# A three-stage transformer kernel: transfers of the expert arms issued by GpSimd, late conversions moved into the last arm, transposes ahead of the second unit

## The chip, the cores and the metric

One Trainium2 chip, one of its cores. The metric is the device time of one execution in microseconds (us). Five engines run their own instruction streams and meet at semaphores: TensorE (PE, with its weight loads PEld), VectorE (DVE), ScalarE (ACT), GpSimd (POOL) and SyncE (SP). SP computes nothing here: it issues transfers. A transfer issued by SP goes to queue q1 (hardware), one issued by POOL to queue q0 (software).

## The reference, cut to what matters

```python
attn_out = softmax(causal(q @ k.T / sqrt(64))) @ v        # B 4, H 12, S 448, D 64
x = attn_out -> rows (1792, 768)

def _moe_ref(x, w_gate, w_output_gate, w1, w2):           # 8 experts, 768 -> 1024 -> 768
    e_idx = np.argmax(x @ w_gate, axis=1)                 # one expert for each row
    for e in range(E):
        h = np.maximum(x[mask] @ w1[e], 0.0)
        out[mask] = gate_w * eom * (h @ w2[e])

def _moe2_ref(x, w_in, w_out):                            # 768 -> 2048 -> 768, weights float64
    h = x @ w_in
    g = h - np.tanh(h)
    return g @ w_out
```

How many rows an expert gets is known only on the chip, so the number of row blocks of each expert is a register value and the extra blocks are conditional. The weights of the second network come as float64 and must be turned into two float16 planes (a high and a low one).

## The kernel before

**Three stages.** Attention runs to about 240 us. The experts follow, one after the other, to about 539 us. Then the second network runs to the end, first as the hidden tiles `fh` (L1358) of row group 0, which DVE and ACT pace, then as `fo` (L1409) and `fh` together, which keep PE full.

**An expert** `e` has one block of 128 rows that is always computed, the main slot `slot(e, FB[e], ...)`, and then nested conditional arms, `extra(e, i)`: each is a `tc.If(cntr > i)` with one more slot in it. A slot is a first product (`ph`, L164), a relu that splits it in a high and a low half (`hh` on ACT L171, `hl` on DVE L172), a second product (`py`, L176) and the result `yo` (ACT L893), which is stored to `ys_d` (L921). All engines branch at an arm (L934). With this input the following arms are taken (the stores of `ys_d` in the trace show it): none for experts 0, 3 and 5, one for experts 1, 4 and 7, two for expert 2, four for expert 6.

**What the main slots carry besides.** While expert `e` is computed, the weights of the next one come in: SP issues 14 loads `raw<-w` (L107) in the order in which they are used, ACT makes the high plane `w` (L115), DVE the low one (L123). SP runs ahead of PE by the three staging buffers `raw`.

**What the arms carry besides.** Each arm converts "units" of the float64 weights: a load `cu<-wf` of 1 MB (`conv_load`, L971), three DVE steps that build a float32 (`to_f32`, L961, L964, L967), the high planes on ACT (L115), the low planes on DVE (L123) or on POOL (`rest_of` with "p": L117 and L131), and a store `wb_d<-co` of 512 KB (`conv_store`, L988). Arms of experts 1 to 5 have two units, those of expert 6 three. There are two load buffers `cu`, so a unit's load is issued when the float32 step of the unit that had the buffer before is done. The third unit of expert 6's arms takes the low planes on POOL. `conv_fill(e, i)` calls these steps at the points `z` = 0 to 4 of the slot. The row numbers of loads and stores come from a table through a register (`unit_of`, L999), read on SP.

**An arm that is not taken.** The program was scheduled as if the arm ran, so each engine that skips it still has to bring the semaphores up to the counts that the transfers in it would have left. In the trace these are the rows of L934: the branch itself, `EVENT_SEMAPHORE` on SP and `INC_SWDGE_SEM` on POOL.

**Expert 7** has no next expert. Its main slot has a `fill` of its own: the last units of the arms, `prep_max` (row maxima, L1064), `first_planes`, `first_hi` and `first_rest`, which prepare row group 0 of the second network (scales, high planes, low planes `prep_lo`, L1092). After its arm comes the **junction** to the second network: the transposes of group 0 (`prep2`: PE L151, copies L153 and L155), the row scales (`prep3`: `rsp`, L1134 and L1135), the two last units (loads into `stg[0]` and `stg[1]`, converted in place), and the scales of group 1 (`prep1`, `prep_sc`, L1072 to L1110, and `prep_hi`, ACT L1084). In the loop behind it, step `a_mm(n)` makes `fh` and `act_a(n)` takes it from PSUM to `cc` (DVE L1366), then ACT L1367 to L1374, POOL L1368 and L1371 and DVE L1378 work on it.

The order of an engine's instructions is the order in which the code is written; nothing reorders them later.

## Time and profile before

| | |
|---|---|
| median of 3 runs | 1016.27 us (1013.7 to 1017.19) |
| profiled execution | 1012.6 us, span 1010.9 us |
| mean granted TensorE clock | 0.989 |
| PE busy | 961.9 us, 95% |
| DVE, ACT, POOL busy | 791.5, 614.3, 480.9 us |

The span is the part of the execution that the trace covers; 1.7 us lie around it. In the trace's lists a row gives its start, its time, the engine, the line, what is written and read, and in brackets how long the engine had been idle before it and what released it. "SPq" or "ACTq" is the engine's own sequencer, that is a branch, a register read or a semaphore step. The granted clock 1.00 is the upper of TensorE's two levels (2.4 GHz), 0.50 the lower (1.2 GHz).

### The profile page before, as it was taken

The numbers are of one execution on the slowest core, as the hardware profiler recorded it, in microseconds if no ns is written. First come the engines' busy times: TensorE is split into PE (matmuls) and PEld (weight loads), VectorE is DVE, ScalarE is ACT, GpSimd is POOL, SyncE is SP. The second block draws the span as 40 slices with busy tenths as digits, with TensorE's granted clock in tenths as the row PEclk, the third lists the DMA queues.
The fourth block names the chain that finished last, engine by engine and source line by source line (L and its number), as shares of the span: only waits on it lengthen the run. The fifth ranks groups of instructions, "written<-read, shape, count | busy, mean of one in ns | idle before, by whom it ended". The sixth has DMA issues, their size and how long they took to land. (4 is left out here: it accounts for less than half of the span.)

```text
span 1010.9 us, 24113 instructions
## 1 busy us (share of the span) xinstructions
PE 961.9 (95%) x9177; PEld 715.8 (71%) x9177; DVE 791.5 (78%) x1740; ACT 614.3 (61%) x1174; POOL 480.9 (48%) x544
## 2 busy tenths in 40 slices
PE   4999999998999999989998899999999999999996
PEld 3998989986878787768684555666666666667764
DVE  7888888977978686876886999886988788686640
ACT  5898988764654556643354897665665665565530
POOL 8668887863211111302255797554534544343321
PEclk9999999999999999989998999999999999999998
DMA  9777787577799989879875340010001000000000
GB/s 243 219 230 215 217 225 191 178 244 252 276 388 347 308 330 352 314 244 344 309 269 226 125 194 17 32 32 10 29 27 33 17 24 8 17 17 16 17 24 24
DMA packets 59831, 166.36 MB, mean 165 GB/s; under 512 B 7920, under 2 KB 21872, under 8 KB 56608
## 3 DMA queue, kind: packets, MB, share of 16 engines
q1 hardware_dynamic: 55120, 144.68, 43.0%
q0 software_dynamic: 4560, 19.80, 5.5%
q8 instruction: 80, 1.31, 0.5%
q14 instruction: 71, 0.58, 0.2%
HBM read 122.21 MB, written 29.62 MB: 150 GB/s over the span
## 5 line engine op out<-in xcount | busy, mean ns | idle before, releaser
L1409 PE MATMUL fo<-wo,g 128*128 128x384 f16 x1344 | 228.2, 326 | 0.0
L1358 PEld LDWEIGHTS <-raw 128*128 128x128 f16 x1440 | 142.2, 99 | 86.9 <-issue 10.3
L1409 PEld LDWEIGHTS <-g 128*128 128x128 f16 x1344 | 131.2, 98 | 83.8
L1368 POOL TENSOR_TENSOR V<-cu,cc 128x384 f32<-128x384 f32 (+1 forms) x80 | 78.5, 982 | 190.7 <-ACT cu L1367 189.7
L164 PEld LDWEIGHTS <-w 128*128 128x128 f16 x2592 | 145.9, 98 | 8.5 <-issue 7.4
L1358 PE MATMUL fh<-cu,raw 128*128 128x384 f16 (+1 forms) x864 | 135.6, 314 | 3.5 <-DVE cc L1366 2.6
L123 DVE SCALAR_TENSOR_TENSOR w<-raw,w 128x768 f16<-128x768 f32 (+1 forms) x99 | 100.2, 1073 | 8.0 <-ACT w L115 8.0
L371 ACT ACTIVATE P<-s,nb 112x112 f32<-112x112 f32 (+1 forms) x192 | 91.5, 510 | 22.2 <-DVE nb L363 20.1
L858 POOL DMA_INDIRECT xg<-xs_d,idx x22 | 32.8, 1490 | 148.5 <-PEq L934 28.6
L115 ACT ACTIVATE w<-raw 128x768 f16<-128x768 f32 (+2 forms) x106 | 90.0, 908 | 12.2 <-DMA raw<-w 10.7
L1367 ACT ACTIVATE cu<-cc 128x384 f32<-128x384 f32 (+1 forms) x80 | 40.1, 501 | 94.1 <-DVE cc L1366 94.1
L363 DVE CUSTOM_DVE_ANT_0 s<-s,maskw 112x112 f32<-112x112 f32 (+1 forms) x192 | 86.2, 455 | 9.6 <-PE s L357 5.5
L1371 POOL TENSOR_TENSOR X<-cc,X 128x384 f32<-128x384 f32 (+1 forms) x80 | 91.2, 1140 | 4.2 <-ACT X L1370 0.5
L1366 DVE TENSOR_TENSOR cc<-fh,co 128x384 f32<-128x384 f32 (+1 forms) x80 | 42.0, 525 | 64.7 <-PE fh L1358 51.9
L1378 DVE SCALAR_TENSOR_TENSOR V<-cu,V 128x384 f32<-128x384 f32 (+1 forms) x80 | 85.1, 1063 | 0.1
L420 PE MATMUL o<-v,PT 112*112 112x65 f32 x576 | 83.9, 269 | 0.0
L1386 DVE TENSOR_TENSOR V<-V,co 128x384 f32<-128x384 f32 (+1 forms) x64 | 78.4, 1224 | 0.0
L1387 ACT ACTIVATE g<-V 128x384 f16<-128x384 f32 (+1 forms) x80 | 40.1, 502 | 47.1 <-DVE V L1386 47.0
L1358 PE MATMUL fh<-yh,raw 128*128 128x384 f16 x384 | 67.6, 326 | 0.7 <-DVE cc L1366 0.7
L420 PEld LDWEIGHTS o<-v,PT 112*112 112x112 f32 x576 | 67.8, 177 | 0.0
L390 PE MATMUL t<-ident,P 112*112 112x112 f32 x480 | 67.0, 262 | 0.0
L356 PE MATMUL s<-kh,qa 128*112 128x112 f16 (+1 forms) x192 | 53.2, 298 | 13.1 <-POOL qa L293 7.1
(678 smaller groups left out, 2096.8 us busy)
## 6 DMA issues: line engine op xcount, KB each, us to landing
raw<-w SPq DMA_DIRECT2D x48, 512.0 KB
raw<-w SPq DMA_DIRECT2D x64, 384.0 KB
cu<-wf SPq DMA_DIRECT2D x22, 1024.0 KB
wb_d<-co SPq DMA_DIRECT2D x22, 512.0 KB
raw<-kq SPq DMA_DIRECT2D x11, 896.0 KB
raw<-wb_d SPq DMA_DIRECT2D x8, 768.0 KB
xs_d<-xq SPq DMA_DIRECT2D x24, 224.0 KB
raw<-v SPq DMA_DIRECT2D x11, 448.0 KB
```

Source lines behind the costliest of these rows:

```text
L115: nc.scalar.activation(out=out, in_=in_, func=AF.Copy, scale=WS)
L123: nc.vector.scalar_tensor_tensor(out=out, in0=in_, scalar=WS, in1=hi, op0=ALU.mult, op1=ALU.subtract)
L164: nc.tensor.matmul(out=ph[:, (f % 4) * 128 : (f % 4 + 1) * 128], lhsT=w[0][:, ww, k, f * 128 : (f + 1) * 128], rhs=xTs[tag][:, xx, k, :], ...
L363: nc.vector.tensor_tensor_reduce(out=d["s", m][:, z, :], in0=d["s", m][:, z, :], in1=maskw[:, S - n : S], scale=-0.125, scalar=3.0e38, op0 ...
L371: nc.scalar.activation(out=d["P"][:, j, OFF[i] : OFF[i] + n], in_=d["s", m][:, z, :], func=AF.Exp, bias=d["nb"][:, 2 * i + j : 2 * i + j + ...
L420: nc.tensor.matmul(out=po[:, i, :], lhsT=d["PT"][:, PT_AT[g], o : o + CP], rhs=d["t"][3][:, hl, j, :], start=(j == 0), stop=(j == i))
L1358: nc.tensor.matmul(out=ph[:, 0:nt], lhsT=wi[ww][:, f // 4, k, f % 4 * 128 : (f % 4 + 1) * 128], rhs=yy[:, k, 0:nt], start=(q == 0), stop=( ...
L1368: nc.gpsimd.tensor_tensor(out=d["V"], in0=d["U"], in1=d["h"], op=ALU.mult)
L1371: nc.gpsimd.tensor_tensor(out=d["X"], in0=d["h"], in1=d["X"], op=ALU.subtract)
L1378: nc.vector.scalar_tensor_tensor(out=d["V"], in0=d[f"S{z}"], scalar=QD[z - 1], in1=d["V"], op0=ALU.add, op1=ALU.mult)
L1386: nc.vector.tensor_tensor(out=d["V"], in0=d["V"], in1=rs_y(g, nt), op=ALU.mult)
L1409: nc.tensor.matmul(out=po[:, 0:384], lhsT=t[:, x, k, i * 128 : (i + 1) * 128], rhs=wo_[ww][:, k, z * 384 : (z + 1) * 384], start=(k == 0 a ...
```

## The change

Three things are edited. In the arms, the loads and stores of the units and the store of the slot's result are issued by POOL and no longer by SP, and the registers for them are read on POOL; a main slot's own store stays on SP. In expert 7, `prep_max(0)` moves from before the first product to point 1 of the main slot, `first_rest` makes all three low planes on DVE (two were on POOL) and moves with the conversion of the first of the two last units into the arm, or into an `Else` branch if the arm isn't taken. At the junction, the transposes of group 0 stand first, then the second of the last units, and the scales of group 1 move behind `act_a(0)` of the loop.

```diff
--- before.py
+++ after.py
@@ -20,6 +20,7 @@
 AX = mybir.AxisListType
 PSUM = bass.MemoryType.PSUM
 SP = mybir.EngineType.SP
+POOL = mybir.EngineType.Pool
 
 B, H, S, D = 4, 12, 448, 64
 CP, NCH = 112, 4
@@ -914,11 +915,12 @@
         out_z(1, py)
         j = i - FB[e]
         if isinstance(j, int) and j == 0:
-            cstr[0] = nc.values_load(cst0[0:1, e : e + 1], engines=(SP,), min_val=0, max_val=NT)
-            r0 = cstr[0]
+            r0 = nc.values_load(cst0[0:1, e : e + 1], engines=(SP,), min_val=0, max_val=NT)
+            nc.sync.dma_start(out=ys_d[ds(r0, 128)], in_=yo)
+            cstr[0] = nc.values_load(cst0[0:1, e : e + 1], engines=(POOL,), min_val=0, max_val=NT)
         else:
-            r0 = nc.snap(cstr[0] + j * 128, engines=(SP,), min_val=0, max_val=NT)
-        nc.sync.dma_start(out=ys_d[ds(r0, 128)], in_=yo)
+            r0 = nc.snap(cstr[0] + j * 128, engines=(POOL,), min_val=0, max_val=NT)
+            nc.gpsimd.dma_start(out=ys_d[ds(r0, 128)], in_=yo)
         fill(4)
 
     cstr = [None]
@@ -931,16 +933,20 @@
     def extra(e, i, w):
         last = FB[e] + LV
         nxt = (i + 1) % 2
-        with tc.If(cntr > i, label=f"more_{e}_{i}"):
+        with tc.If(cntr > i, label=f"more_{e}_{i}") as more:
             hint(e, i + 1)
             if i > last:
                 beyond(e, i, w)
                 return
             if e == E - 1 and 1 < i < last:
                 slot_rows(e, i + 1, 0)
-            slot(e, i, w, i % 2, conv_fill(e, i), trans=((0, nxt),) if i < last else (),
+            slot(e, i, w, i % 2, last_fill if e == E - 1 and i == 1 else conv_fill(e, i), trans=((0, nxt),) if i < last else (),
                  then=(lambda: slot_rows(e, i + 2, 0),) if i + 1 < last and e + 1 < E else (), late=True)
             extra(e, i + 1, w)
+        if e == E - 1 and i == 1:
+            with more.Else():
+                for z in range(5):
+                    last_fill(z)
 
     def beyond(e, i0, w):
         icol = mt.tile([128, 1], U32, name=f"icol_{e}", tag="icol", bufs=1)
@@ -984,8 +990,8 @@
 
     stores = []
 
-    def conv_store(b, r):
-        st = nc.sync.dma_start(out=wb_d[:, :, ds(r, 1), :].rearrange("p a o n -> p a (o n)"), in_=co[b]).ins
+    def conv_store(b, r, eng=nc.sync):
+        st = eng.dma_start(out=wb_d[:, :, ds(r, 1), :].rearrange("p a o n -> p a (o n)"), in_=co[b]).ins
         tc.declare_no_dep(st, group="units", reason="each unit has a place of its own in wb_d")
         tc.add_to_no_dep_group("units", st)
         stores.append(st.name)
@@ -995,8 +1001,8 @@
             tc.add_manual_dep(ins, n, mybir.DependencyInfo(mybir.DependencyClass.Sync, mybir.DependencyReason.DATA),
                               reason="reads what the stores of the units wrote")
 
-    def unit_of(e, n):
-        return nc.values_load(xtab[0:1, UOFF[e] + n : UOFF[e] + n + 1], engines=(SP,), min_val=0, max_val=NDY - 1)
+    def unit_of(e, n, eng=SP):
+        return nc.values_load(xtab[0:1, UOFF[e] + n : UOFF[e] + n + 1], engines=(eng,), min_val=0, max_val=NDY - 1)
 
     def conv_fill(e, i):
         c = CPE[e] if e + 1 < E else 0
@@ -1010,8 +1016,8 @@
                 if z == at:
                     conv(cu[b], co[b][:, 0], co[b][:, 1], "p" if j == 2 else "v")
                 if z == (4 if at == 3 else at):
-                    conv_load(cu[b], unit_of(e, n0 + j + min(c, 2)))
-                    conv_store(b, unit_of(e, n0 + j))
+                    conv_load(cu[b], unit_of(e, n0 + j + min(c, 2), POOL), nc.gpsimd)
+                    conv_store(b, unit_of(e, n0 + j, POOL), nc.gpsimd)
 
         return fill
 
@@ -1156,8 +1162,8 @@
         prep_dg(0, 0, GB[0])
 
     def first_rest():
-        for j in range(GB[0] - 1):
-            prep_lo(0, 0, GB[0], j, "p")
+        for j in range(GB[0]):
+            prep_lo(0, 0, GB[0], j)
 
     def rows_again(step):
         for g in range(2):
@@ -1253,11 +1259,8 @@
             second = nc.values_load(flg[0:1, 0:1], engines=(SP,), min_val=0, max_val=128)
             remaining()
             qc = (cc, wof[0][:, 8192:10240].bitcast(U32))
-            prep_max(0, 0, GB[0], (0, 1))
 
             def fill(z):
-                if z == 0:
-                    prep_max(0, 0, GB[0], (2,))
                 if z == 2:
                     first_hi()
                 if z in (1, 2):
@@ -1267,10 +1270,28 @@
                 if z == 1:
                     for q in range(2):
                         conv_load(stg[q], NDY + q, nc.gpsimd)
+                    prep_max(0, 0, GB[0])
                     first_planes()
                 if z == 3:
+                    prep_max(1, 0, GB[1])
+
+            qhl = [[y[:, (10 + q) * 1024 : (11 + q) * 1024] for y in wof] for q in range(2)]
+
+            def last_f32(q):
+                to_f32([(qc[q][:, h], stg[q][:, h, :]) for h in HS])
+
+            def last_planes(q):
+                for z in range(2):
+                    for h in HS:
+                        c = qc[q][:, h].bitcast(F32)
+                        scaled("a", qhl[q][0][:, h], c) if z == 0 else rest_of("p", qhl[q][1][:, h], c, qhl[q][0][:, h])
+
+            def last_fill(z):
+                if z == 1:
+                    last_f32(0)
                     first_rest()
-                    prep_max(1, 0, GB[1])
+                if z == 2:
+                    last_planes(0)
 
         slot(e, FB[e], wts[e], f"n{e % 2}", fill,
              ((1, (FB[e] + 1) % 2),) + ((("n", f"n{(e + 1) % 2}"),) if e + 1 < E else ()),
@@ -1306,23 +1327,12 @@
         extra(e, 1 + FB[e], wts[e])
         if e == 0:
             conv_load(cu[1], unit_of(1, 1))
-    qhl = [[y[:, (10 + q) * 1024 : (11 + q) * 1024] for y in wof] for q in range(2)]
-    prep_lo(0, 0, GB[0], GB[0] - 1)
-    for q in range(2):
-        to_f32([(qc[q][:, h], stg[q][:, h, :]) for h in HS])
-        for z in range(2):
-            for h in HS:
-                c = qc[q][:, h].bitcast(F32)
-                scaled("a", qhl[q][0][:, h], c) if z == 0 else rest_of("p", qhl[q][1][:, h], c, qhl[q][0][:, h])
-        if q == 0:
-            for prep in (prep2, prep3):
-                for i in range(GB[0]):
-                    tpool[0] = (mp_t, mp_y, mp_h)[i]
-                    prep(0, i, "tys"[i])
-    prep1(1, 0, GB[1], False, False)
-    prep_sc(1, 0, GB[1])
-    for j in (2, 0, 1):
-        prep_hi(1, 0, GB[1], j)
+    for prep in (prep2, prep3):
+        for i in range(GB[0]):
+            tpool[0] = (mp_t, mp_y, mp_h)[i]
+            prep(0, i, "tys"[i])
+    last_f32(1)
+    last_planes(1)
 
     mctx.close()
     gt = [w16s[1][z].tile([128, 2, KF2, 384], F16, tag=tg, name=f"g_{z}") for z, tg in enumerate(("w1", "w2"))]
@@ -1443,6 +1453,11 @@
             act_c(n - 2, 1)
         if okf(n - 3):
             act_d(n - 3)
+        if n == 0:
+            prep1(1, 0, GB[1], False, False)
+            prep_sc(1, 0, GB[1])
+            for j in (2, 0, 1):
+                prep_hi(1, 0, GB[1], j)
         if n in (1, 2, 3):
             prep_lo(1, 0, GB[1], (2, 0, 1)[n - 1])
         if n == 4:
```

The first rows are SP's, at the end of expert 5's main slot and at its first arm; `cst_82` is the register of the main slot's store, `xtab` the table of unit numbers. Before:

```order
L107 DMA raw_90<-w 128x768 x8
L917 TENSOR_LOAD cst_82
L917 ISA x2
L921 ISA
L921 DMA ys_d<-yo_I-14134_14135 128x768
L934 COMPARE_AND_BRANCH
L929 REGISTER_ALU
L1511 BRANCH_PREFETCH_HINT
L999 TENSOR_LOAD xtab
L999 ISA x2
L971 ISA
L971 DMA cu_4988<-wf 128x2048
```

The same place in the changed kernel:

```order
L108 DMA raw_90<-w 128x768 x8
L918 TENSOR_LOAD cst_82
L918 ISA x2
L919 ISA
L919 DMA ys_d<-yo_I-14184_14185 128x768
L936 COMPARE_AND_BRANCH
L931 REGISTER_ALU
L1526 BRANCH_PREFETCH_HINT
```

SP's arms are empty now: behind these rows stand only the branches of the further arms, and then the loads for the next expert but one.

The second place is POOL's stream at the end of expert 6's first arm: the low planes of the third unit. Before:

```order
L858 DMA xg_4589<-xs_d,idx 128x1536
L117 TENSOR_SCALAR scm<-cc 128x512
L131 TENSOR_TENSOR co_4991<-scm,co_4991 128x512
L117 TENSOR_SCALAR scm<-cc 128x512
L131 TENSOR_TENSOR co_4991<-scm,co_4991 128x512
L934 COMPARE_AND_BRANCH
```

In the changed kernel:

```order
L994 DMA wb_d<-co_5002 256x1x1024
L118 TENSOR_SCALAR scm<-cc 128x512
L132 TENSOR_TENSOR co_5001<-scm,co_5001 128x512
L118 TENSOR_SCALAR scm<-cc 128x512
L132 TENSOR_TENSOR co_5001<-scm,co_5001 128x512
L922 ISA
L923 DMA ys_d<-yo_I-16475_16476 128x768
L1005 TENSOR_LOAD xtab
L1005 ISA x2
L977 ISA
L977 DMA cu_4998<-wf 128x2048
```

The load for the next arm and the store of the slot's rows now stand behind the low planes on the engine that makes them.

The third place is DVE's stream at the junction (`cu_4989` is the transposed group, `wo_18065` the second of the last units, `wo_18066` the scales). Before:

```order
L1092 SCALAR_TENSOR_TENSOR wo_18066<-raw_90,wo_18066 128x6x128
L961 TENSOR_SCALAR cc<-wo_18065 128x512 x2
L964 SCALAR_TENSOR_TENSOR cc<-wo_18065,cc 128x512 x2
L967 SCALAR_TENSOR_TENSOR cc<-wo_18065,cc 128x512 x2
L153 COPY cu_4989<-pt_I-19833_19834 128x6x128
L153 COPY cu_4989<-pt_I-19851_19852 128x6x128
L153 COPY cu_4989<-pt_I-19869_19870 128x6x128
L961 TENSOR_SCALAR wo_18065<-wo_18065 128x512 x2
L964 SCALAR_TENSOR_TENSOR wo_18065<-wo_18065 128x512 x2
L967 SCALAR_TENSOR_TENSOR wo_18065<-wo_18065 128x512 x2
L1072 TENSOR_TENSOR wo_18066<-wo_18066,smt 128x3
```

In the changed kernel:

```order
L1098 SCALAR_TENSOR_TENSOR wo_18136<-raw_90,wo_18136 128x6x128
L936 UNCONDITIONAL_BRANCH
L154 COPY cu_4999<-pt_I-19917_19918 128x6x128
L154 COPY cu_4999<-pt_I-19935_19936 128x6x128
L154 COPY cu_4999<-pt_I-19953_19954 128x6x128
L967 TENSOR_SCALAR wo_18135<-wo_18135 128x512 x2
L970 SCALAR_TENSOR_TENSOR wo_18135<-wo_18135 128x512 x2
L973 SCALAR_TENSOR_TENSOR wo_18135<-wo_18135 128x512 x2
L1376 TENSOR_TENSOR cc<-fh_20029,co_5001 128x384
L1078 TENSOR_TENSOR wo_18136<-wo_18136,smt 128x3
```

The first unit's three float32 steps and a low plane are gone from in front of the copies, and the first `act_a` now stands ahead of the scales of group 1 instead of behind them.

## Rows read from the trace of the kernel before

**Rows 1.** Line 934 on SP, from 425 to 440 us, and who waited.

```profile
L934 SPq EVENT_SEMAPHORE  x9: 17/17/17, 435.9 to 438.2; - x9
...
L934 SPq COMPARE_BRANCH  x1: 65/65/65, 430.6 to 430.6; - x1
...
  ACT yo_I-16038_16039 L893: 5.0, 1
```

**Rows 2.** Timeline of ACT behind the untaken arms of expert 3.

```profile
379.38 0.49 ACT L893 ACTIVATE yo_I-12244_12245<-py_I-12433_12434 128x384 f32<-128x384 f32 x1 [6.91 <-SPq L934]
```

**Rows 3.** Timeline of PE, the stalls behind the arms of experts 3 and 5.

```profile
385.16 0.50 PE L176 MATMUL py_I-12809_12810<-w,hh_I-12600_12601 128*128 128x384 f16 x2 [1.04 <-ACT hh_I-12600_12601 L171]
386.43 0.34 PE L176 MATMUL py_I-12809_12810<-w,hl_I-12602_12603 128*128 128x384 f16 x1 [0.77 <-DVE hl_I-12602_12603 L172]
...
443.65 0.82 PE L176 MATMUL py_I-16610_16611<-w,hh_I-16401_16402 128*128 128x384 f16 x2 [3.65 <-ACT hh_I-16401_16402 L171]
```

**Rows 4.** Stretches of 5 us: us, PE busy, granted clock, DMA share, GB/s.

```profile
440.00:445.00 5.00, 0.89 (x3) 0.73 0.89 278
445.00:450.00 5.00, 5.00 (x19) 0.59 0.80 270
```

**Rows 5.** Line 934 over the span, GpSimd's part (ns min/median/max).

```profile
L934 POOLq INC_SWDGE_SEM  x8: 355/592/822, 251.0 to 537.1; - x8
```

**Rows 6.** Timeline of SP in expert 6's arms, three of its loads.

```profile
452.50 0.34 SPq L971 DMA_DIRECT2D cu<-wf  x1
...
467.60 0.35 SPq L971 DMA_DIRECT2D cu<-wf  x1
...
478.67 0.34 SPq L971 DMA_DIRECT2D cu<-wf  x1
```

**Rows 7.** Timeline of DVE there: first steps of units.

```profile
457.57 0.43 DVE L961 TENSOR_SCALAR cc<-cu 128x512 uint32<-128x512 uint32 x1 [2.70 <-DMA cu<-wf]
...
475.47 0.76 DVE L961 TENSOR_SCALAR cc<-cu 128x512 uint32<-128x512 uint32 x2 [1.56 <-DMA cu<-wf]
...
481.56 1.04 DVE L961 TENSOR_SCALAR cc<-cu 128x512 uint32<-128x512 uint32 x1
...
486.70 0.75 DVE L961 TENSOR_SCALAR cc<-cu 128x512 uint32<-128x512 uint32 x2
...
497.77 0.98 DVE L961 TENSOR_SCALAR cc<-cu 128x512 uint32<-128x512 uint32 x2
```

**Rows 8.** Timeline of POOL: last low plane of the second arm's third unit.

```profile
481.15 1.16 POOL L131 TENSOR_TENSOR co<-scm,co 128x512 f16<-128x512 f32 x1
```

**Rows 9.** Timeline of PE: starts of expert 6's second arm and expert 7.

```profile
454.46 0.33 PE L164 MATMUL ph_I-16757_16758<-xT,w 128*128 128x128 f16 x3
...
504.86 0.23 PE L164 MATMUL ph_I-18122_18123<-xT_n,w 128*128 128x128 f16 x1 [0.73 <-PEq L934]
```

**Rows 10.** Line 971: POOL's own two loads (ns), and their landing.

```profile
L971 POOL DMA_DIRECT2D wo<-wf x2: 577/626/676, 523.1 to 523.8; - x2
...
DMA to landing us min/median/max: 6.0/7.3/8.5
```

**Rows 11.** Timeline of DVE: before the junction, and act_a(1).

```profile
539.29 1.02 DVE L1092 SCALAR_TENSOR_TENSOR wo<-raw,wo 128x768 f16<-128x768 f32 x1 [7.25 <-ACTq L934]
...
555.06 0.56 DVE L1366 TENSOR_TENSOR cc<-fh,co 128x384 f32<-128x384 f32 x1 [1.25 <-PE fh L1358]
```

**Rows 12.** The chain that ended last, in order of time, at the junction.

```profile
543.39 1.40 DVE cu L153 x3
544.78 1.36 DVE wo L961 x2
...
549.50 0.50 DVE wo L1072
```

**Rows 13.** Timeline of PE: the first hidden tile.

```profile
546.48 0.80 PE L1358 MATMUL fh<-cu,raw 128*128 128x384 f16 x2 [0.93 <-ACT co L1135]
```

**Rows 14.** The page, part 5: matmuls of hidden tiles (busy, mean ns, idle).

```profile
L1358 PE MATMUL fh<-cu,raw 128*128 128x384 f16 (+1 forms) x864 | 135.6, 314 | 3.5 <-DVE cc L1366 2.6
```

## The prediction, made before the changed kernel had run

> **What bounds the kernel now.** I read the chain that ended last first: it is TensorE's at the end, so time can only come from places where PE stands still or runs at the lower clock. Then I read PE's idle time in the list of instructions, and behind each stall the engine that it waited for. Three places matter here.
>
> The first is expert 5's arm that isn't taken. SP branches at 430.6, and from then until 438.2 it does nothing but bring up semaphores, nine steps that wait for transfers still under way [rows 1]. The reader is to see 7.6 us in which SP issues no weight load. ACT waits 5.0 us for that [rows 1], its relu half is late, and PE's second product starts 3.65 us late [rows 3]. The clock falls with it: 0.73 in the stretch from 440 and 0.59 in the next [rows 4], although PE is busy for all of the latter. The same happens behind expert 3's arm, milder: ACT waits 6.91 us on SP [rows 2], PE 1.04 and 0.77 us, one stall for each half of the relu [rows 3].
>
> The second is expert 6's four arms, each with three units, where DVE and the loads set the pace. From the second arm's start at 454.46 to expert 7's at 504.86 three arms took 50.4 us [rows 9], 16.8 each. DVE's own round, from the first step of a unit to the same one an arm later, is 481.56 to 497.77, 16.21 us, and it waits for loads twice, 2.70 and 1.56 us [rows 7].
>
> The third is the junction. DVE stands idle 7.25 us before 539.29 because the low planes behind it come after the branch [rows 11]. Then, in the chain, it makes a float32 before the copies of the transposed rows (543.39), and another one behind them until 549.50 [rows 12]; PE's first hidden tile starts only at 546.48 [rows 13].
>
> **The arms' transfers leave SP.** What is removed: SP's skip of an empty arm. SP now walks past the branches of the untaken arm and goes on with weight loads 7.6 us earlier at expert 5. I cost this by PE's stalls, not by SP's wait, since PE lags behind SP. Expert 3: 1.04 + 0.77 = 1.8 us. Expert 5: the stall of 3.65 us, and the clock after it. At 0.59 the stretch from 445 gives away 5 x 0.41 = 2.05 us, and half of the 0.89 us in which PE worked before it, 0.45 [rows 4]. Together 6.15 us. The bounds are nothing and all of it. I take all: the waits end on SP by name, and a stall on a slow engine's queue has no other work queued before it there.
>
> What is added: POOL must do the skip. Its version shows in the row of `INC_SWDGE_SEM`, 0.36 to 0.82 us, 8 times [rows 5]. With transfers of its own in the arms it gets waits for them as well, as SP had. Behind them stand its gathers, which fetch the rows of a slot ahead of the slot that uses them. So I cost POOL's skip at nothing; the cover is one slot, and if it were gone, POOL's 7.6 us would be PE's. That is a rival below.
>
> **The price: expert 6's arms.** Here the transfers are really issued, seven in an arm, and POOL also makes the third unit's low planes. SP issued the next load of that buffer at 478.67 [rows 6]; DVE used it at 486.70 [rows 7]. On POOL this load stands behind the low planes, which end at 481.15 + 1.16 = 482.31 [rows 8], and behind the issue of the slot's rows, 0.63 us by the mean of POOL's two loads [rows 10]: 482.94. The register read on POOL has no row; between nothing and one more issue of 0.63 I count half, 0.3. So 483.25, 4.6 us later than SP.
>
> How long it then takes has three rows. From SP's issue to the first step of DVE that waited for it, 452.50 to 457.57, that is 5.07 us, and 467.60 to 475.47, that is 7.87 us [rows 6, 7]. POOL's own two landed in 6.0 and 8.5 us [rows 10], the second behind the first. The load in question comes with only the rows' store ahead of it, so it is nearest to 5.07 and 6.0, and I take 5.5, between them. It lands at 488.75, 2.05 us after DVE wants it. DVE's round becomes 16.21 + 2.05 = 18.26, three arms 54.8, against 50.4: a cost of 4.4 us. At 5.07 the cost is 3.1, at 7.87 it is 11.5 (483.25 + 7.87 = 491.1, 4.4 late, 20.6 an arm); if the load were never late, the arms could at best run at DVE's 16.21 and give 1.8 back. The stall falls on DVE, so the next thing late is the relu's low half, then PE.
>
> One rule speaks against the move beyond this. The Trainium skill, in "SBUF — State Buffer", section "SBUF: two separate sides", warns that a transfer issued by GpSimd needs descriptors which GpSimd can't write while DVE holds their shared port in one of its two-port modes; it gives 620 ns alone and 3,100 ns beside a DVE copy. The trace of before has only two plain loads from POOL, and their issue took 0.58 and 0.68 us [rows 10], which shows no such hold; whether DVE was in such a mode then, no row shows. By the page's figures the two issues that stand before the load would cost 5 us more in each arm, 15 in three, and the kernel would be slower by some 7.5 us.
>
> **Expert 7.** `prep_max` of group 0 is only later on DVE, under PE's second product; nothing, since DVE's work behind it is needed at the junction, where it has 7.25 us of slack [rows 11]. `first_rest` and the float32 of the first of the last units go into that slack: three low planes of 1.02 us [rows 11] and a float32 that took from 539.29 + 1.02 = 540.3 to 543.39, 3.1 us [rows 12], 6.2 in all, under 7.25. That holds if the unit has landed by then; it is issued by POOL at 523.1 and lands 6.0 or 8.5 us later [rows 10], at 532 at the latest.
>
> **The junction.** The copies can start when DVE is through with the low plane, about 540.3 instead of 543.39: 3.1 us. The first hidden tile goes from 546.48 [rows 13] to about 543.4. The first two tiles then took until 555.06, when `act_a(1)` waited for the second [rows 11], 8.6 us; at the mean rate of the group, 135.6 us for 864 matmuls [rows 14], 36 of them need 5.65. DVE's other work: the second float32 took 544.78 to 549.50, 4.7 us [rows 12], and follows the copies, 541.7 to 546.4. Then `act_a(0)`, 0.56, as soon as the first tile is there (543.4 + 2.8 at the mean rate, 546.2, or + 4.3 at the slow one, 547.7), then the scales of group 1. Those began at 549.50 [rows 12] and ended 1.25 + 0.56 us before 555.06, at 553.25 [rows 11], so 3.75 us. `act_a(1)` comes at 546.4 + 0.56 + 3.75 = 550.7 or 547.7 + 0.56 + 3.75 = 552.0, instead of 555.06: 3.1 to 4.4 us. I take the middle, 3.8. It carries through, because the loop behind it is paced by DVE and ACT and not by PE. POOL's low planes of the second unit move with the float32.
>
> **Sum.** 1.8 + 6.15 + 3.8 - 4.4 = 7.35 us. The profiled execution took 1012.6; 1005.25 by it. It lies 3.7 below the median of the runs shown, 1016.27, and I forecast the median: 1008.9 us.
>
> **The rivals.**
>
> *POOL-issued loads are slow, and expert 6's arms set the time (slower).* If POOL's loads land in 8.5 us [rows 10], the third unit's comes 483.25 + 8.5 - 486.70 = 5.05 late, and the one that SP landed in 7.87 another 0.63. An arm takes 16.21 + 5.7 = 21.9, three 65.7, 15.3 more than now. The sum is 11.75 - 15.3 = -3.5: 1019.8. If the load that took 5.07 is hit too, 3.4 more: 1023. It decides from (50.4 + 11.75) / 3 - 16.21 = 4.5 us of lateness an arm. For it: both of POOL's landings are longer than 5.07, and the rule above. Against: the 8.5 is the second of two megabytes issued 0.7 us apart.
>
> *The load takes 7.87 (same).* 11.75 - 11.5 = 0.25: 1016.
>
> *The skip only changes its engine (the change doesn't do what it should; same).* POOL waits as long as SP did, and gathers or PE's rows come late by it. Then the 7.95 us of experts 3 and 5 stay: 3.8 - 4.4 = -0.6, 1016.9. For it: the waits belong to transfers, not to SP. Against: the gathers are a slot ahead.
>
> *The load is hidden (faster).* Expert 6's arms stay at 16.8: 11.75, 1004.5; with DVE's 16.21 another 1.8.
>
> **How the numbers follow.** About 0.3%, 3 us, is what a measurement can tell from no change: under 1013.2 is faster, over 1019.3 slower. Chances: the forecast 0.43 (1005 to 1013), the load hidden 0.18, the load at 7.87 0.13, the skip that stays 0.10, slow loads from POOL 0.16. Faster: 0.43 less 0.02 for its edge, 0.18, and 0.04 of the third and fourth, where the junction gives more: 0.63. Slower: 0.11 of the last and 0.02 of each same case, 0.15. Same: 0.22. The best bounds give 1.8 + 6.15 + 4.4 + 1.8 = 14.15, 1002.1; the range goes from there to 1019.5, which leaves out the slow loads' upper half and little else. The likeliest case's own range is 1005 to 1013.
>
> **What would show it.** SP's row of the branch at expert 5 has no string of semaphore steps behind it, and raw loads follow at once; the 440 to 450 stretch has a clock near 1.00. In expert 6's arms DVE shows a new wait on `cu<-wf` of about 2 us once an arm; arms of 18.3. At the junction the copies come first and `act_a(1)` some 4 us after them earlier than now, relative to the end of expert 7. Wrong would be: PE stalls that stay behind experts 3 and 5, now named after POOL; DVE waits over 4.5 us in an arm; a lower clock in the arms.

## The result, and the profile after

| | before | changed |
|---|---|---|
| median, 17 runs each | 1013.7 us (1009.44 to 1020.5) | 1027.2 us (1017.54 to 1030.68) |
| profiled execution, span | 1012.6, 1010.9 | 1027.59, 1026.1 |
| ratio to before | | 1.0107, 95% interval 1.0082 to 1.0132 |

The change makes the kernel 1.1% slower; I had forecast 0.7% faster. The changed kernel's runs lie in two groups, seven from 1017.5 to 1021.5 and ten from 1026.9 to 1030.7. The profile is one of the upper group.

The first view of the changed kernel is PE's list of waits over the whole span (us in total, times, longest).

```profile
PE pt_I-16256_16257 L152 <- DMA xg<-xs_d,idx: 7.4, 1, 7.4
...
PE pt_I-9008_9009 L152 <- DMA xg<-xs_d,idx: 5.6, 1, 5.6
...
PE fh L1368 <- DMA raw<-wb_d: 3.9, 1, 3.9
```

None of the three was there before. Two are waits for `xg`, the rows that GpSimd gathers for a slot; one is at the junction. The stalls of [rows 3] behind experts 3 and 5 are gone, and so is SP's string of semaphore steps of [rows 1]: at expert 5's arm SP now has a branch and nothing behind it. The same line, from 428 to 440 us:

```profile
L936 POOLq EVENT_SEMAPHORE  x5: 17/43/43, 433.3 to 436.1; - x5
L936 SPq COMPARE_BRANCH  x1: 59/59/59, 428.7 to 428.7; - x1
L936 POOLq INC_SWDGE_SEM  x1: 1098/1098/1098, 436.2 to 436.2; - x1
```

The skip has gone to GpSimd, where it costs a wait as well. What it delays shows in GpSimd's timeline from expert 4's first arm on:

```profile
397.49 0.58 POOL L977 DMA_DIRECT2D cu<-wf  x1 [3.31 <-DMA raw<-w]
399.19 0.72 POOL L994 DMA_DIRECT2D wb_d<-co  x1 [1.13 <-DVE cc L967]
410.96 0.56 POOL L923 DMA_DIRECT2D ys_d<-yo_I-12654_12655  x1 [11.04 <-ACT xT L156]
412.30 0.54 POOL L977 DMA_DIRECT2D cu<-wf  x1 [0.78 <-issue]
413.84 0.68 POOL L994 DMA_DIRECT2D wb_d<-co  x1 [1.00 <-DVE w L124]
425.53 1.02 POOL L859 DMA_INDIRECT xg<-xs_d,idx  x1 [11.01 <-issue]
426.85 1.41 POOL L859 DMA_INDIRECT xg<-xs_d,idx  x1 [0.31 <-issue]
```

Eleven us go by before the arm's store of its rows, and eleven more between the arm's last store and the next gather. PE wanted the rows of the second of these gathers in expert 6's main slot. The chain that ended last, in order of time, names the two waits:

```profile
397.92 12.38 DMA ys_d<-yo_I-12284_12285
...
413.84 23.34 DMA wb_d<-co
...
438.18 4.15 DMA xg<-xs_d,idx
```

The first piece is not the arm's own store. It is the main slot's, which SP issued at 397.92 and which landed 12.4 us later; the arm's store on GpSimd waits for it. The second piece runs on through GpSimd's next skip, of expert 5's arms.

I read the start of the first product of each slot from PE's timeline and took differences. That gives where the 15.2 us between the two spans lie (e2x1 is expert 2's first arm; `fh` and `fo` are the first hidden tile and the first output tile):

```
us, from - to           before   changed   late edits alone (below)
start - e1              254.74    255.52    256.95
e1 - e2x1                52.20     52.17     52.19
e2x1 - e2x2              16.51     24.60     16.51   a gather is late
e2x2 - e4x1              51.79     51.79     51.80
e4x1 - e5                19.28     17.12     18.88   SP's skip of expert 3 is gone
e5 - e6                  19.02     17.50     17.50
e6 - e6x1                17.58     27.02     19.82   a gather is late
e6x1 - e6x2              23.34     16.51     21.24   SP's skip of expert 5 is gone
e6x2 - e7                50.40     55.52     50.39   three arms of expert 6
e7 - e7x1                17.15     19.73     16.52
e7x1 - fh                24.47     24.92     20.93   the junction
fh - fo                  65.80     67.22     61.78
fo - end                398.62    396.48    398.59
```

Where I had priced gains there are gains, 2.2 and 6.8 us; the first is not shown to be the skip's (see the part on the prediction). The price of expert 6's arms is there: 5.1 us. What I had not priced are the two late gathers, 8.1 and 9.4 us. Each is PE's wait and, behind it, a lower granted clock: 1.00 from 280 to 305 us, and from 305 to 325 the row reads (us, PE busy, clock, DMA share, GB/s)

```profile
305.00:325.00 20.00, 14.45 (x182) 0.86 0.97 379
```

And the junction gave nothing. The first hidden tile ([rows 13] before) waits there for the float16 planes, because a store that they need is late. The first view is of SP's queue: two stores of planes between 541.1 and 553.6 us, and the loads of the planes behind them; the second is PE's wait.

```profile
541.09 12.52 SPq L994 DMA_DIRECT2D wb_d<-co  x2
...
556.22 3.83 SPq L1044 DMA_DIRECT2D raw<-wb_d  x5
```

```profile
562.40 0.82 PE L1368 MATMUL fh<-cu,raw 128*128 128x384 f16 x2 [3.85 <-DMA raw<-wb_d]
```

### The profile page after: what moved, and what is told of

Its sections match the earlier page's. It is cut to its first block, busy times and chain, and to the rows that moved or that the text cites. A ratio compares the mean times of both kernels' runs of the same rounds, so it can differ in the third digit from the quotient of the medians.

```text
span 1026.1 us, 24134 instructions
## 1 busy us (share of the span) xinstructions
PE 965.1 (94%) x9177; PEld 717.4 (70%) x9177; DVE 790.5 (77%) x1742; ACT 613.1 (60%) x1174; POOL 504.1 (49%) x585
## 4 chain that ended last, share of the span: by engine, by line
PE 40%; DMA 10%; issue 5%; ACT 4%; DVE 3%; POOL 1%; POOLq 1%; DVEq 0%; SPq 0%; ACTq 0%
PE fo L1419 21%; PE fh L1368 17%; DMA wb_d<-co 5%; DMA cu<-wf 2%; DMA ys_d<-yo_I-12284_12285 1%; DMA raw<-wb_d 1%; DMA xg<-xs_d,idx 1%; ACT S L1379 1%; POOL co L132 1%; DVE cc L970 1%; ACT cu L1377 1%; ACT X L1380 0%; ACT g L1397 0%; DVE cc L967 0%; DVE V L1396 0%
```

## The experiments

Theory A was that GpSimd, which takes its instructions in the order of the code, holds its gathers behind the arms' transfers and the skip. The rivals were B, that the late edits cost the time; C, that transfers from GpSimd are slow in themselves; D, that a skip only changes its engine.

### The two halves of the change

`arms_only` is before with this alone, `late_only` the changed kernel without it:

```diff
-        nc.sync.dma_start(out=ys_d[ds(r0, 128)], in_=yo)
+            nc.gpsimd.dma_start(out=ys_d[ds(r0, 128)], in_=yo)
...
-                    conv_load(cu[b], unit_of(e, n0 + j + min(c, 2)))
-                    conv_store(b, unit_of(e, n0 + j))
+                    conv_load(cu[b], unit_of(e, n0 + j + min(c, 2), POOL), nc.gpsimd)
+                    conv_store(b, unit_of(e, n0 + j, POOL), nc.gpsimd)
```

> Only the arms' transfers move to GpSimd; expert 7 and the junction are as before. Theory A (GpSimd is one queue in order: its gathers stand behind the arm's store, which waits for SP's store of the main slot to land, and behind the skip, which waits for its own transfers): the two gathers come late as in the changed kernel, PE stands 5 to 7 us at each in experts 2 and 6, expert 7 starts 11 to 13 us late and nothing behind it gives that back: 0.9 to 1.3% slower than before. Theory B (the loss comes from the edits in expert 7 and at the junction): no more than 0.3% off the time before. Theory C (transfers from GpSimd are slow in themselves): slower too, but the lateness grows by every unit, also in expert 1's and 4's arms, and not in two steps.

> Only the edits in expert 7 and at the junction; the arms' transfers are SP's as before. Theory A: expert 7 starts when it did before, and the 3.8 us that I forecast for the junction show, at least in part: between the time before and 4 us less. Theory B: 5 to 10 us more than before, at the junction. The wait of the first hidden tile for the loads of the float16 planes, 3.85 us in the changed kernel, tells which: by A it comes from late stores and is gone here, by B it stays.

Measured: `arms_only` 1.0121 (1.0073 to 1.0169), `late_only` 0.9902 (0.987 to 0.9935), 1005.3 us. B falls. The late edits alone are 1% faster, more than the 4 us that I had expected; the arms' transfers are the whole loss. The profile of `arms_only`, its slowest execution, has both stalls, 5.7 and 7.1 us, as theory A said; expert 7 starts 22 us later than before, where I had expected 11 to 13. In `late_only` the wait for the planes is gone and the first hidden tile starts without one:

```profile
542.41 0.33 PE L1357 MATMUL ro<-wo,onesb 128*128 128x128 bf16 x3
542.73 14.94 PE L1367 MATMUL fh<-cu,raw 128*128 128x384 f16 x90
```

The clock was lower here before (us, PE busy, clock, DMA share, GB/s):

```profile
545.00:550.00 5.00, 4.08 (x16) 0.50 0.93 380
```

It is now 1.00 through the whole stretch:

```profile
540.00:545.00 5.00, 4.59 (x50) 1.00 0.39 104
545.00:550.00 5.00, 5.00 (x33) 1.00 0.98 399
550.00:555.00 5.00, 5.00 (x32) 1.00 0.15 59
```

### Which experts' arms cost it

All three are `late_only` with some arms on GpSimd:

```diff
+    ON_POOL = (0, 3, 5)      # or (1, 4), or (6,)
+    arm_eng = lambda e: (POOL, nc.gpsimd) if e in ON_POOL else (SP, nc.sync)
```

> The late edits, and the arms of experts 0, 3 and 5 alone on GpSimd. With this input none of these arms is taken, so GpSimd issues no transfer of theirs and SP skips nothing there. Theory A (untaken arms are cheap on GpSimd as long as it has nothing of its own under way; the loss comes from taken arms): SP's string of semaphore steps at these experts is gone, PE's stalls behind experts 3 and 5 with it, no gather is late: 3 to 7 us less than the late edits alone, so 1.3 to 1.7% faster than before. Theory D (the skip is a wait for transfers and only changes its engine): equal to the late edits alone within 2 us, 0.8 to 1.2% faster than before.

> The late edits, and the arms of experts 1 and 4 alone on GpSimd. One arm of each is taken and the rest is skipped. Theory A: GpSimd waits for its own store and load to land before it is through the skip, the gathers behind it come late, PE waits 5 to 7 us for rows in expert 6's main slot and in part of the executions in expert 2's: 5 to 15 us more than the late edits alone, so between 0.5% faster and 0.5% slower than before. Theory C (each transfer from GpSimd costs the same): four units of all the thirty-odd cost little, within 3 us of the late edits alone.

> The late edits, and the arms of expert 6 alone on GpSimd: ten slots' worth of units less none, all arms taken. Theory A: each load that follows GpSimd's own low planes comes some 2 us late, 4 to 6 us in the three arms, and 2 to 4 more in expert 7, whose gather and first unit stand behind them: 6 to 10 us more than the late edits alone, so 0 to 0.4% faster than before. If the arms are as long as SP's, the price that I put on them in the prediction was wrong.

Measured: `pool_035` 0.9889 (0.9866 to 0.9913), `pool_14` 1.0136 (1.01 to 1.0171), `pool_6` 1.0078 (1.0051 to 1.0105). So two experts with one taken arm each cost 2.4% against `late_only`, 21.5 us between the medians; C had allowed them 3, and theory A itself 5 to 15. GpSimd's timeline of `pool_14` behind expert 4's arm:

```profile
404.29 0.35 SPq L919 DMA_DIRECT2D ys_d<-yo_I-12254_12255  x1
```

```profile
416.73 0.56 POOL L924 DMA_DIRECT2D ys_d<-yo_I-12624_12625  x1 [13.59 <-ACT w L116]
418.14 0.54 POOL L980 DMA_DIRECT2D cu<-wf  x1 [0.85 <-issue]
420.33 0.68 POOL L997 DMA_DIRECT2D wb_d<-co  x1 [1.65 <-DVE xT_n L154]
434.31 1.02 POOL L859 DMA_INDIRECT xg<-xs_d,idx  x1 [13.29 <-issue]
```

The first row is SP's, the main slot's store. Two waits stand in series, 13.59 and 13.29 us, and PE waited 8.3 us for rows in expert 2 and 12.3 in expert 6. Against that, the untaken arms cost GpSimd nothing: in `pool_035` the same line at expert 5's place has

```profile
L939 POOLq INC_SWDGE_SEM  x1: 702/702/702, 420.0 to 420.0; - x1
```

and no gather is late. But the 5.6 us that `pool_035` gains from expert 6's main slot to its second arm (35.5 against 41.1 us) it gives back in the three arms behind (56.7 against 50.4): it is only 0.1% under `late_only`, short of theory A's numbers and within theory D's. (Its profile is of its slowest execution, 3.6 us over its median, so the others may give back less.) `pool_6` cost more than I expected, 1.8% over `late_only`: 5.8 us in its arms, and then 2.4 in expert 7 and 5.9 up to the first hidden tile.

### A rule that needs no knowledge of the input

```diff
+    arm_eng = lambda e, i: (SP, nc.sync) if i == 1 + FB[e] or e >= E - 2 else (POOL, nc.gpsimd)
```

> The late edits; of experts 0 to 5 the first arm's transfers are SP's and those of arms 2 to 4 GpSimd's, experts 6 and 7 all on SP. A rule that needs no knowledge of the input. With this input GpSimd then issues transfers in one arm only (expert 2's second). Theory A: GpSimd has nothing under way when it skips, so no gather is late but at most one; SP skips one arm instead of five and waits for fewer transfers: 0 to 5 us less than the late edits alone, so 1.0 to 1.5% faster than before. Theory D: the wait is for the latest transfers under way and not for their number, so SP loses as much as before: equal to the late edits alone.

Measured: 0.9928 (0.9905 to 0.995), 1.4 us over `late_only` in the median, where theory A had 0 to 5 us less and theory D no difference. Expert 7's arm starts 6.0 us earlier than in `late_only` (515.80 against 521.80, with starts at expert 1 that agree within 0.2), and the first hidden tile 1.5 later: the gain is given back in expert 7's arm, where PE waits 3.98 us for ACT, and at the junction; why these are longer is not shown.

### Mending the first wait, and expert 6

`ys_pool` is the changed kernel with the main slot's store on GpSimd, `six_on_sp` the changed kernel with expert 6's arms on SP, `ys_pool_six_sp` has both (the first in experts 0 to 5); `pool_14_ys` is `pool_14` with the first.

```diff
-            nc.sync.dma_start(out=ys_d[ds(r0, 128)], in_=yo)
+            nc.gpsimd.dma_start(out=ys_d[ds(cstr[0], 128)], in_=yo)
...
+            eng, dma = (SP, nc.sync) if e == E - 2 else (POOL, nc.gpsimd)
```

> The changed kernel, and the main slot's own result store is issued by GpSimd as well, so that the arm's store no longer waits for a store that SP queued behind weight loads. Theory A: GpSimd's 11.0 us in front of the arm's store in expert 4 and 7.3 us in expert 1 go or fall under 3 us, the gathers behind come 5 to 10 us earlier, and PE's two stalls (5.6 and 7.4 us) go wholly or mostly: 10 to 16 us less than the changed kernel, so 0 to 0.6% faster than before. Theory C: one more transfer from GpSimd for every expert, as slow as the changed kernel or slower.

> The changed kernel, but the transfers in expert 6's arms are SP's again (they are all taken with this input). Theory A: the three arms of expert 6 go back to the 50.4 us of before from 55.5, so 5 us less than the changed kernel, and the two stalls at the gathers stay: still 0.4 to 0.8% slower than before. Theory C: as most of GpSimd's units are in expert 6, most of the loss goes: within 0.3% of before.

> The changed kernel with both mends: the arms of expert 6 on SP, and in experts 0 to 5 the main slot's result store on GpSimd. Theory A: the arms of expert 6 take 50 to 52 us and expert 7 starts as early as in the kernel with expert 6 on SP; the stall in expert 2 is gone in all executions and the one in expert 6's main slot, 6.8 us, is halved at least, unless the first gather behind the skip is stretched as it was with all stores on GpSimd (7.3 us): 4 to 8 us less than with expert 6 on SP alone, 0.5 to 1.1% faster than before. If the skip alone is enough to delay the gathers, as with expert 6 on SP alone, 0.2%.

> As the kernel with the arms of experts 1 and 4 alone on GpSimd, and the main slot's result store of these two experts is GpSimd's too. Theory A: there GpSimd lost 12 and 13.6 us at the arm's store, which waited for SP's store of the main slot, and then 12.5 and 13.3 us at the skip. The first of the two waits falls to 2 or 3 us, so the gathers come some 10 us earlier; of PE's waits for rows, 8.3 and 12.3 us, nothing and 2 to 5 are left: 10 to 18 us less than that kernel, 0.3% slower to 0.5% faster than before. Theory C (transfers from GpSimd are slow in themselves): two more of them, no gain.

Measured: `ys_pool` 0.9981 (0.9958 to 1.0004), `six_on_sp` 0.9982 (0.9948 to 1.0016), `ys_pool_six_sp` 0.9917 (0.9891 to 0.9942), `pool_14_ys` 1.0043 (1.0024 to 1.0062). Each mend takes 1.2% from the changed kernel, both together 1.9%. Theory C had no gain for `ys_pool`, and falls there. In `ys_pool` GpSimd waits 2.0 us at the arms' stores of experts 1 and 4, and PE's stall in expert 2 is gone; in expert 6 PE still waits 6.5 us, behind a gather that took 7.32, and so it does in the profile of `ys_pool_six_sp`, its slowest execution (6.5, 7.29). `six_on_sp` did more than the 5 us that theory A gave it, and its total is the one that C gave it; its three arms are back at 50.5 us, and its profile shows no late gather in expert 2. Its runs lie in two groups, 1006.8 to 1010.3 and 1016.5 to 1020.8, and the profile is of the lower. That the groups are the late gather in expert 2, there or not, fits both kernels, but I have no profile of each group of one kernel.

In `pool_14_ys` the wait at the arm's store fell from 13.59 to 1.99, as expected, and the total by 0.9%, 8.9 us between the medians, a little less than I expected: PE still waits 6.3 and 6.7 us for rows. GpSimd's timeline shows what took its place:

```profile
407.05 0.56 POOL L924 DMA_DIRECT2D ys_d<-yo_I-12604_12605  x1 [1.99 <-ACT yo_I-12604_12605 L894]
408.95 0.54 POOL L980 DMA_DIRECT2D cu<-wf  x1 [1.34 <-DVEq L939]
410.56 0.69 POOL L997 DMA_DIRECT2D wb_d<-co  x1 [1.07 <-issue]
423.99 7.15 POOL L859 DMA_INDIRECT xg<-xs_d,idx  x1 [12.74 <-issue]
```

The wait at the skip stayed, and the first gather behind it took 7.15 us; in `pool_14` it took 1.02.

### What the skip waits for, and the load behind GpSimd's own work

`pool_14_loads` and `pool_14_stores` give back to SP one half of the units' transfers of `pool_14_ys`; `pool_6_early` issues the third unit's load ahead of GpSimd's low planes:

```diff
+                    to_f32([(cc[:, h], cu[b][:, h, :]) for h in HS])
+                    conv_load(cu[b], unit_of(e, n0 + j + min(c, 2), eng), dma)
+                    conv_planes(cc, co[b][:, 0], co[b][:, 1], "p")
```

> As the kernel with the arms of experts 1 and 4 and their main slots' stores on GpSimd, but the stores of the units are SP's; loads and stores of rows stay GpSimd's. If GpSimd's wait of some 13 us at the skip is for the last of its own transfers to land, it shrinks only by what the last store adds, 0 to 5 us, and PE still waits 3 to 7 us in experts 2 and 6: within 6 us of that kernel.

> The other half: the loads of the units are SP's, their stores and the stores of rows GpSimd's. If the skip waits for the last of GpSimd's own transfers, the 13 us shrink by the megabyte that no longer stands ahead of the last store, 3 to 8 us, and PE's waits for rows with them: 3 to 10 us less than with both on GpSimd. If the time of the skip doesn't depend on what GpSimd has under way, nothing changes in either half.

> As the kernel with expert 6's arms alone on GpSimd, but GpSimd issues the third unit's next load right behind that unit's float32, ahead of its own low planes and of the rows' store. By the price in the prediction (the load stands 4.6 us later because of what GpSimd does before it) the load is issued about 4 us earlier, DVE's waits for it shrink by 2 to 3 us an arm and the three arms come within 2 us of SP's 50.0: 4 to 8 us less than that kernel. By the rival (loads that GpSimd issues land late wherever they stand, 6 to 8.5 us) DVE waits as long for the other units and the gain is under 3 us.

Measured: `pool_14_loads` 0.9983 (0.9963 to 1.0002), 0.6% under `pool_14_ys`; `pool_14_stores` 0.9942 (0.992 to 0.9964), 1.0% under it; `pool_6_early` 1.0012 (0.9989 to 1.0036). With half of GpSimd's transfers gone, its idle time ahead of the gather behind expert 4 is 11.75 (loads left) and 9.45 us (stores left) instead of 12.74, and PE waits for no rows in experts 2 and 6 in either. For `pool_14_loads` I had expected that it still would. The gather is not only earlier there: it takes 1.35 us and not 7.15. So the skip's wait does depend on what GpSimd has under way, by 1 to 3 us; the larger part of what the gather gained, 5 to 6 us, is that it was no longer stretched. Which of the transfers the skip waits for is not shown.

`pool_6_early` takes 0.7% from `pool_6`. The three arms fall from 56.2 to 51.1 us, DVE's waits for loads between 455 and 520 us from

```profile
DVE cc L970 <- DMA cu<-wf: 10.2, 6, 3.3
```

to

```profile
DVE cc L970 <- DMA cu<-wf: 4.9, 4, 1.4
```

In these arms it is the place in GpSimd's queue that costs the time, not the issuer. The kernel as a whole stays 1.1% over `late_only`: in its profile 4.0 us of that lie between expert 4's first arm and expert 5, whose transfers the two kernels issue alike. Why is not shown.

### What in the late edits gives the gain

`scales_before` puts the scales of group 1 back ahead of `act_a(0)`; `unit_late` puts the low planes and the first of the last units back ahead of the transposes:

```diff
+    prep1(1, 0, GB[1], False, False)
+    prep_sc(1, 0, GB[1])
...
+    first_rest()
+    last_f32(0)
+    last_planes(0)
```

> The late edits, but the scales of group 1 stand at the junction again, ahead of the first act_a. By my sum for the junction the scales are 3.75 us of DVE that then stand in front of act_a(0) and not behind it; the second float32 is done before the first hidden tile is: 2 to 4 us more than the late edits alone, 0.6 to 0.8% faster than before. If the gain comes from the clock alone, which the late edits kept at 1.00 through the junction, no difference.

> The late edits, but the three low planes of group 0 and the first of the last units stand at the junction again, ahead of the transposes. By my sum they cost what the arm hides, 3.1 us of low planes and 3.1 us of float32 before the copies can start, and PE is idle for as long: 5 to 8 us more than the late edits alone, 0.2 to 0.5% faster than before; the clock falls to 0.50 behind the junction as it did before. If the order at the junction gives the gain and not what the arm hides, within 2 us of the late edits alone.

Measured: `scales_before` 0.9964 (0.9941 to 0.9987), `unit_late` 1.0002 (0.9982 to 1.0022); 6 and 10 us over `late_only` by the ratios, where I had expected 2 to 4 and 5 to 8. In the stretches that the edits touch the profiles give less: `scales_before` loses 3.6 us between the first hidden and the first output tile, `unit_late` 5.4 up to the first hidden tile and 0.9 behind it, both as expected; the rest does not lie there. Both parts are needed: without either, most or all of the late edits' gain is gone. In `scales_before` the clock is 1.00 in each 5 us from 540 to 560 and the time is lost all the same, so the clock alone does not make the gain. In `unit_late` PE waits 3.0 us at the row scales again, and the clock falls behind it:

```profile
545.00:550.00 5.00, 2.51 (x11) 0.72 0.93 364
550.00:555.00 5.00, 5.00 (x20) 0.60 0.24 102
```

## Why the prediction was wrong, step by step

**The gains behind the untaken arms: expert 5's right, expert 3's not shown.** For expert 5, 6.15 us forecast, 6.8 measured, and 5.6 in `pool_035`, where no gather is late. For expert 3, 1.8 forecast and 2.2 measured. But SP skips nothing there in `pool_035` and `arms_only` either, and the stretch from expert 4's first arm to expert 5 took 19.2 and 22.6 us in their profiles, against 19.28 before. In `pool_035` ACT and PE wait as in [rows 2] and [rows 3], and ACT's wait has another name:

```profile
357.00 13.03 SPq L108 DMA_DIRECT2D raw<-w  x14
...
382.15 0.49 ACT L894 ACTIVATE yo_I-12264_12265<-py_I-12453_12454 128x384 f32<-128x384 f32 x1 [7.03 <-DMA ys_d<-yo_I-10364_10365]
387.92 0.50 PE L177 MATMUL py_I-12829_12830<-w,hh_I-12620_12621 128*128 128x384 f16 x2 [0.99 <-ACT hh_I-12620_12621 L172]
389.19 0.34 PE L177 MATMUL py_I-12829_12830<-w,hl_I-12622_12623 128*128 128x384 f16 x1 [0.77 <-DVE hl_I-12622_12623 L173]
```

The main slots share one buffer for their results (`bufs=1`). ACT can write expert 4's only when the store of expert 3's has landed, and SP issued that store at 371.3, behind fourteen weight loads. I had taken the skip for the cause because it was the last to end. `ys_pool`, whose GpSimd issues this store at 362.0, has neither wait. Nor is such a gain kept: what expert 5 gave came back in expert 6's arms in `pool_035`, where DVE waits 7.5 us for loads between 425 and 510 us against 4.0 in `late_only`, and in expert 7's arm and at the junction in `first_arm_sp`.

**GpSimd's skip at nothing: this is the step that failed.** I wrote that its gathers fetch the rows of a slot ahead of the slot that uses them, so that the cover is one slot. I looked at untaken arms only. There the price is nothing, as `pool_035` shows (0.70 us). Behind a taken first arm GpSimd has its own transfers under way. In the changed kernel the arm's store waits for the main slot's store on the other queue (11.0 us in expert 4, 7.3 in expert 1), then the skip behind the arm's last store takes 11.0 and 9.3 us, and in expert 1 the gather itself took 5.7 us. The cover of one slot, some 17 us, is less than such a sum; PE paid 8.1 and 9.4 us for what I had put at nothing. `pool_14` shows this alone, and `pool_14_ys`, `pool_14_loads` and `pool_14_stores` take it away piece by piece. The third rival had the mechanism and the wrong size: it lost the gain and no more, and it let GpSimd wait where SP had waited, at the untaken arms. The first rival's "slower" came true by luck: it was to come from expert 6's arms, 15.3 us, and these cost 5.1.

**Expert 6's arms: right in kind.** 4.4 us forecast, 5.1 measured in the changed kernel and 5.8 in `pool_6`, and `pool_6_early` shows that it is the load's place. The waits lie where I put one and at a second load too; in the changed kernel around the third arm, rows that answer to [rows 7]:

```profile
479.22 0.84 DVE L967 TENSOR_SCALAR cc<-cu 128x512 uint32<-128x512 uint32 x2 [2.37 <-DMA cu<-wf]
...
485.10 0.76 DVE L967 TENSOR_SCALAR cc<-cu 128x512 uint32<-128x512 uint32 x2 [1.11 <-DMA cu<-wf]
...
499.06 0.76 DVE L967 TENSOR_SCALAR cc<-cu 128x512 uint32<-128x512 uint32 x2 [2.52 <-DMA cu<-wf]
```

I did not follow the lateness on into expert 7: 2.6 us in its main slot.

**The junction: right order, wrong size, and then lost.** 3.8 us forecast up to `act_a(1)`; alone, in `late_only`, the first hidden tile starts 3.5 us earlier after expert 7's arm, `act_a(1)` 5.5 (549.38 against the 555.06 of [rows 11]) and the first output tile 7.6. I had taken the middle between PE's mean and its slow rate, while the clock stayed at 1.00, and the scales took 2.95 us and not 3.75. And my sum ended at `act_a(1)`. The 3.6 us that `scales_before` loses lie behind it: there `act_a(0)` comes 3.1 us later than in `late_only`, right ahead of an `act_a(1)` that is as early, and DVE then waits for what POOL makes of the first tile. `late_only`, then `scales_before`:

```profile
545.96 0.56 DVE L1375 TENSOR_TENSOR cc<-fh,co 128x384 f32<-128x384 f32 x1 [0.61 <-POOL scm L118]
...
549.38 0.55 DVE L1375 TENSOR_TENSOR cc<-fh,co 128x384 f32<-128x384 f32 x1
```

```profile
549.03 1.01 DVE L1379 TENSOR_TENSOR cc<-fh,co 128x384 f32<-128x384 f32 x2
551.97 1.37 DVE L1391 SCALAR_TENSOR_TENSOR V<-S,V 128x384 f32<-128x384 f32 x1 [1.94 <-POOL V L1381]
```

In the changed kernel the late stores of expert 7 took all of it: the condition that I had named, that the unit has landed in time, hid a second one, that the planes of the first hidden tile are stored in time.

**The rule of the Trainium skill.** "SBUF — State Buffer", section "SBUF: two separate sides", would have a transfer of GpSimd held while DVE is in one of its two-port modes. In expert 6's arms the issues took 0.54 to 0.76 us in the changed kernel, beside DVE's work, and the arms cost 5.1 us, where the rule would have put 15 on top of the 4.4: no such hold there. Whether DVE was in such a mode, no row shows. For gathers see below.

## What to carry to other kernels

Before moving transfers to an engine that also issues something else, list what stands behind them in its queue for the taken branch and for the untaken one; the taken branch with a skip behind it was the worst case here. Stores to one tensor from two queues waited for each other here: keep them on one. When a wait ends on one engine by name, ask what else it would have waited for a moment later. And measure the halves of a change apart: here one half was worth 1%, and the other cost 1.2% alone and 2% on top of the first. No kernel here is clearly faster than `late_only` (0.9902): `pool_035` (0.9889) lies 0.1% under it, every other one over it.

## What I had not expected of the hardware

Most gathers took 0.9 to 2 us. In all the traces of this study eight took over 5 us, and each of the eight lies beside an unbroken run of nine of DVE's low planes (L123 of before, 8.2 us) and ends 0.8 to 0.9 us after that run. One of them is in the kernel before, 413.75 to 418.93, where DVE's run ends at 418.12. In `pool_14_ys` DVE's row beside the gather at 423.99 is

```profile
422.10 8.16 DVE L124 SCALAR_TENSOR_TENSOR w<-raw,w 128x1024 f16<-128x1024 f32 x9
```

It ends at 430.26, the gather at 431.14. Ten kernels, before among them, have one more gather of 3.6 us, between 254 and 260 us, beside a run of four (254.14 to 257.70 before), and it too ends 0.8 us after the run. That reads like the rule of the Trainium skill, "SBUF — State Buffer", section "SBUF: two separate sides": a transfer of GpSimd held while DVE has the port that they share. But the run alone does not do it: other gathers lie wholly inside runs of nine and took 1.0 to 1.8 us, as this one of before, with DVE's run beside it:

```profile
358.28 1.48 POOL L858 DMA_INDIRECT xg<-xs_d,idx  x1 [2.32 <-PEq L934]
```

```profile
355.99 8.16 DVE L123 SCALAR_TENSOR_TENSOR w<-raw,w 128x1024 f16<-128x1024 f32 x9
```

In `pool_14_loads` three gathers, of 1.74, 1.40 and 1.76 us, lie inside one such run (414.68 to 422.85). What tells the two kinds apart no run here shows, so the cause stays open. That the gathers stand ahead of the skip was not tried.
